# Whole token loads, a new order of the first key products, and w1's column means from rounded parts, in a one-core attention and mixer kernel

## The chip, the core and the metric

The kernel runs on one core of a Trainium2 chip. The metric is the device time of one execution in microseconds (us). The kernel before takes 523.48 us, the median of three runs (523.04 to 523.54).

The core has five engines that run their own instruction queues and meet at semaphores: TensorE (PE in the profile; PEld are its weight loads), VectorE (DVE), ScalarE (ACT), GpSimd (POOL) and SyncE (SP). SP and POOL also issue the DMA transfers between memory and the core's on-chip buffers; TensorE writes to accumulation banks (PSUM), which VectorE and ScalarE read.

## The reference

Two blocks read the same normalized tokens; one gates the other. There are S = 2048 tokens of D = 512 features, 32 heads of 16, and F = 1376 hidden features.

```python
xn = layernorm(x)
# A: linear attention
q, k, v = split(xn @ wqkv)
pq, pk = phi(q), phi(k)          # phi(t) = t + 1 if t > 0 else exp(t), plus 1e-6
kv  = einsum("bhsd,bhse->bhde", pk, v);  z = sum over s of pk
s   = (pq @ kv / (pq . z + 1e-6)) @ wo
# B: token mixing by shifts, then an MLP
h   = gelu(layernorm(xn) @ w1)   # its four column groups shifted by +1, -1, +2, -2 tokens
x1  = xn + shifted(h) @ w2
b   = x1 + gelu(layernorm(x1) @ w3) @ w4
out = x + s * silu(b)
```

## The kernel before

**Precision and tiling.** Tokens are cut into 16 tiles of 128, four tiles to a block of 512; the 512 features are cut into four chunks of 128. Nearly all products are made from rounded parts: a matrix a is split into hi (a rounded to the fp32r format, `rounded` at L478 or `Weights.split` at L552; usually ScalarE's copy) and lo (a - hi, VectorE's subtraction), and a product is the sum of hi*hi, hi*lo and lo*hi (`products`, L470): three TensorE instructions for each chunk. A product of unrounded values (`slow=True`) is one instruction that TensorE runs in two passes.

**A planner, not a scheduler of the chip, orders the work.** The code first records every operation with `Plan.add`. `Plan.emit` (L267) then lays them out in time by a table of assumed costs and emits them; the order of each engine's queue is what it decides. It works from due times (`deadlines`, L240, and `backward`, L261, which for a load takes an assumed latency off its user's due time; `PATIENCE` is the slack of operations that touch PSUM). The last lines of the kernel nudge single operations (the table `SOONER`, pairs of an operation's number and quarters of a microsecond) and set how early an operation may take a buffer (`lead`, `reserve`) and how far TensorE's order may depart from the order of recording (`window`, `ahead`).

**The start (L1176 to L1222).** TensorE runs WARM = 3 products of ones (`warm`), then one product of ones and zeros (`k<-zacc,ones`) that opens the bank of tile 0. The weights wk of the keys are loaded chunk by chunk (`wk_s`), chunk 0 in two halves of 256 columns. The tokens of block 0, transposed (`xt`), are loaded by `load_u(0, 2)` in two halves of 256 tokens: for every chunk first the half that holds tiles 0 and 1, later the half of tiles 2 and 3. Each half is rounded into u_0h to u_3h and u_0l to u_3l (the number is the chunk). The key products of tiles 0 and 1 begin with chunk 0 unrounded (`raw_k`, L670, tile 0 in two column halves), so that they need not wait for the rounding. Then come chunk 0 for tiles 2 and 3, chunks 1, 2, 3 for tiles 0 and 1, `ksum` (the column sums of wk, a product with ones of VectorE's three-step sum wkt), and chunks 1 to 3 for tiles 2 and 3.

`feature_k` (L738) makes phi(k): VectorE subtracts the mean's part (kt, with wneg, ScalarE's negative of ksum), ScalarE makes relu and exp (kr, kt), VectorE joins them (kr), ScalarE rounds (k0h for tile 0), VectorE takes the rest (k0l). `gram` (L774) then accumulates x^T phi(k) over all tiles in four banks g. The mean and variance of the first four tiles come from two ScalarE passes (sq) over the row-wise tokens x. `WQ.center` (L565) subtracts the column means from the query weights: VectorE sums the four chunks (wqt), one unrounded product with ones spreads the sum (wqm), and VectorE subtracts it from each chunk (wq_s), which is then rounded (wq_0h, wq_0l and so on) for `query`.

`W1.center(by_dma=True)` does the same for the mixer's w1, but the sum w1t is made by a load and three accumulating loads of the POOL queue; the product is w1m.

**The rest** (block by block the mixer, its second product, the MLP with seven products instead of eight per pair of halves, the attention's readout and the gate) is not touched by name, though the planner orders it anew.

**Queues.** SP issues all plain loads and stores in one queue. It uses eight semaphores in turn, so that its ninth transfer waits until the first has landed. POOL issues the accumulating transfers.

Of the kernel before, what the change touches and what calls it, by code (L numbers as in the profile page):

```python
# [14 lines left out]
P = 128  # L15
# [70 lines left out]
class Plan:  # L86
# [138 lines left out]


    GAP = .06
    PATIENCE = 2.5
    COLD, COLD_TILL = 1.84, 5.8
    SAFE = 2.0  # L230
    early = 0.0
# [8 lines left out]
    def deadlines(self, first):  # L240
# [8 lines left out]
        for op in self.ops:  # L249
# [3 lines left out]
            elif any(t.psum for t in op.tiles):  # L253
                op.due = min(op.due, op.at + self.PATIENCE)
            elif op.soon:
# [5 lines left out]
    def backward(self):  # L261
        for op in reversed(self.ops):
            if op.eng != "PE":
                for o in op.post:
                    op.due = min(op.due, o.due - self.GAP - (5.0 + op.mb * 4 if op.mb else op.lat))

    def emit(self, first, lead, reserve, window, ahead, table=()):  # L267
        self.deadlines(first)
# [125 lines left out]
def linear_attn_gated_by_mixer(  # L394
# [18 lines left out]
    NC = D // P  # L413
    NT = S // P
    QT = 4
    NQ = NT // QT
    BT = QT * P
# [1 line left out]
    W = 4  # L419
    SHIFT = (-1, 1, -2, 2)  # L420
    ORDER = (0, 2, 1, 3)
    WARM = 3
    PIECE = BT + W
    EARLY = (), ()
    AHEAD = 30.0, 20.0, 10.0, 0.0, 0.0
    TH = BT // 2
# [11 lines left out]
    pl = Plan(nc, pools, counts, ("acc", "mm"))  # L438

    def piece(name, dt=F32):  # L440
        return pl.new("p", name, dt, PIECE)[:, :512]

    def rounds(name):

        return piece(name + "h", F32R), piece(name + "l", F32R)
# [4 lines left out]
    def bank(name):  # L450
        return pl.new("mm", name, F32, 512)[:, :]

    def fixed(name, n, dt=F32):

        t = pl.new("const", name, dt, n)
        t.ap = const.tile([P, n], dt, name=name)
        return t
# [9 lines left out]
    def split(out, full, hi):  # L467
        pl.tt(out, full, hi.f32, ALU.subtract)

    def products(ps, terms, start=True, stop=True, more=False, behind=None):  # L470

        ms = []
        for sh, sl, mh, ml in terms:
            ms += [(sh, mh), (sh, ml), (sl, mh)]
        for n, (s, m) in enumerate(ms):
            pl.mm(ps, s, m, start and n == 0, stop and n == len(ms) - 1, more=more, behind=None if n else behind)

    def rounded(hi, lo, full, src=None):  # L478

        pl.act(hi, src or full, AF.Copy)  # L480
        split(lo, full, hi)
# [9 lines left out]
    ident, ones, nhalf, zacc = fixed("ident", P), fixed("ones", P), fixed("nhalf", QT), fixed("zacc", 512)  # L491
    identr = fixed("identr", P, F32R)
    onesr, bmask, tiny, zmore = fixed("onesr", P, F32R), fixed("bmask", P), fixed("tiny", 1), fixed("zmore", 1)
# [39 lines left out]
    X, XT = {}, {}  # L533
# [5 lines left out]
    class Weights:  # L539


        def __init__(self, name, src, parts=1):

            self.name, self.src = name, src
            self.raw = [piece(f"{name}_s{c}") for c in range(NC)]
            for c in range(NC):
                n = 1 if c else parts
                for k in range(n):
                    cs = k * 512 // n, (k + 1) * 512 // n
                    pl.load(self.raw[c].cols(*cs), src[:, c, cs[0]:cs[1]])  # L550

        def split(self, shared=0):  # L552
            self.hl = [rounds(f"{self.name}_{c}") for c in range(NC)]
# [11 lines left out]
        def center(self, by_dma=False):  # L565

            t, r = piece(self.name + "t"), self.raw
            if by_dma:
                pl.load(t, self.src[:, 0])
                for c in range(1, NC):  # L570
                    pl.gather(t, self.src[:, c])
            else:
                pl.tt(t, r[0], r[1], ALU.add)
                pl.tt(t, t, r[2], ALU.add)
                pl.tt(t, t, r[3], ALU.add)
            ps = bank(self.name + "m")
            pl.mm(ps, ones.all, t, True, True, slow=True)
            for c in range(NC):
                pl.stt(r[c], ps, -1.0 / D, r[c], ALU.mult, ALU.add)

# [15 lines left out]
    def scale_x(lo, n):  # L596

        r = rs1[:, lo:lo + n]
        w = small(f"w{lo}", n).all
        pl.ts(w, var(mv1, lo, lo + n), EPS, None, ALU.add, eng="POOL")  # L600
        power(r, w, n)
        pl.ts(ns1[:, lo:lo + n], r, -1.0, None, ALU.mult, eng="POOL")
        pl.tt(nm1[:, lo:lo + n], means(mv1, lo, lo + n), ns1[:, lo:lo + n], ALU.mult, eng="POOL")
        for i in range(lo, lo + n):
            halves_x(i)
# [25 lines left out]
    UT = {}  # L631

    def load_u(b, parts):

        n = BT // parts
        UT[b] = [[pl.new("p", f"u{b}_{c}{k}", F32R, PIECE) for k in "hl"] for c in range(NC)]
        for q in range(parts):
            o = q * n
            for c in range(NC):
                if q == 0:  # L640
                    XT[b, c] = piece(f"xt{b}_{c}")
                src = XT[b, c].cols(o, o + n)
                pl.load(src, xt[b, c][:, o:o + n])
                hi, lo = (t[:, 2 + o:2 + o + n] for t in UT[b][c])
                if b == c == q == 0:
                    pl.ts(hi, src, 1.0, None, ALU.mult)
                    split(lo, src, hi)
                else:
                    rounded(hi, lo, src)
# [12 lines left out]
    def ut(b, c, a, z):  # L662
        return tuple(t[:, a:z] for t in UT[b][c])

    def project(ps, i, ws, cs):
        b, j = divmod(i, QT)
        a = 2 + j * P
        products(ps, [ut(b, c, a, a + P) + ws.chunk(c) for c in cs], 0 in cs, NC - 1 in cs)

    def raw_k(ps, i):  # L670

        v = XT[0, 0].cols(i * P, (i + 1) * P)
        if i:
            pl.mm(ps, v, WK.raw[0], True, False, slow=True)
        else:
            for k in range(2):
                cs = k * TH, (k + 1) * TH
                pl.mm(ps.cols(*cs), v, WK.raw[0].cols(*cs), False, False, slow=True)

    def sum_k(ps):  # L680

        t, r = piece("wkt"), WK.raw
        pl.tt(t, r[0], r[1], ALU.add)
        pl.tt(t, t, r[2], ALU.add)
        pl.tt(t, t, r[3], ALU.add)
        pl.mm(ps, ones.all, t, True, True, slow=True)
# [51 lines left out]
    def feature_k(i, ps):  # L738

        t, r = piece(f"kt{i}"), piece(f"kr{i}")  # L740
        pl.stt(t, wneg.all, mean(mv1, i), ps, ALU.mult, ALU.add)
        pl.act(r, t, AF.Relu, scale=col(rs1, i))
        pl.act(t, t, AF.Exp, scale=col(rs1, i))
        hi, lo = rounds(f"k{i}")
        pl.stt(r, t, 1.0, r, ALU.min, ALU.add)
        pl.act(hi, r, AF.Identity, bias=tiny.all)
        pl.stt(lo, r, TINY, hi.f32, ALU.add, ALU.subtract)
        pl.gather(zacc.all, r)
        GK[i] += (hi, lo)

    def key(i):
        ps = bank(f"k{i}")
        project(ps, i, WK, range(NC))
        feature_k(i, ps)
# [421 lines left out]
    warm = bank("warm")  # L1176
    for n in range(WARM):
        pl.mm(warm.cols(n % NC * P, (n % NC + 1) * P), ones.all, ones.all, True, True, slow=True)
    ks = [bank("k0")]
    pl.mm(ks[0], ones.all, zacc.all, True, False, slow=True)  # L1180

    wneg = fixed("wneg", 512)
    G = [pl.new("acc", f"g{c}", F32, 512) for c in range(NC)]
# [12 lines left out]
        pl.act(t, X[i], AF.Square, bias=s.cols(1, 2), total=v)  # L1196
        pl.ts(v, v, 1.0 / D, None, ALU.mult)

    WK = Weights("wk", wqkv[1], 2)
    load_u(0, 2)  # L1200
    WK.split(1)
    for i in range(QT):
# [1 line left out]
    scale_x(0, 1)  # L1204
    scale_x(1, 1)
    scale_x(2, 2)
    ks[1:] = [bank(f"k{i}") for i in range(1, QT)]
    ksum = pl.new("acc", "ksum", F32, 512).all
    for i in range(2):
        raw_k(ks[i], i)  # L1210
    for i in range(2, QT):
        project(ks[i], i, WK, [0])
    for c in range(1, NC):
        for i in range(2):
            project(ks[i], i, WK, [c])
    sum_k(ksum)
    pl.act(wneg.all, ksum, AF.Copy, scale=-1.0)
    for i in range(2):
        feature_k(i, ks[i])
    for i in range(2, QT):  # L1220
        project(ks[i], i, WK, range(1, NC))
        feature_k(i, ks[i])  # L1222
    WQ = Weights("wq", wqkv[0])
    WQ.center()
# [73 lines left out]
    b = NQ - 1  # L1298
# [6 lines left out]
    for base, s in ((0, 1), (DH - 1, -1)):  # L1305
        v = bmask.all.via(lambda ap: ap.rearrange("p (h d) -> p h d", d=DH))
# [16 lines left out]
    for gg in range(NC):  # L1323
        cs = gg * P, (gg + 1) * P
        ps = bank(f"kv{gg}").cols(0, P)
# [4 lines left out]
    for gg in range(NC):  # L1330
        ps = bank(f"m{gg}")
# [10 lines left out]
    for b in range(NQ):  # L1342
# [50 lines left out]
        else:  # L1393
# [3 lines left out]
            t = piece(f"xi{i}", F32R)  # L1397
# [13 lines left out]
                gate(b * QT + QT - 1, a, o, D // 2, late=True, by_dma=False, whole=o > 0)  # L1411

    SOONER = (
# [7 lines left out]
    )  # L1421
    pl.emit(first=6.0, lead={"p": 12.0, "w": 10.0, "ab": 10.0}, reserve={"p": 8, "w": 1, "ab": 0}, window=7.0,
            ahead=3.0, table=SOONER)


# [35 lines left out]
```

## Time and profile before

| | |
|---|---|
| median of three runs | 523.48 us |
| the profiled execution: its own time | 523.29 us |
| its span, first to last instruction | 521.5 us |
| moved by DMA | 100.11 MB, mean 192 GB/s |
| TensorE instructions | 3011 |

One execution was profiled, and 1.8 us of its time lie around the span. In the lines shown below a group or instruction is named by source line, engine, operation and out<-in with buffer numbers left out; since every operation is recorded in a helper, the line is that of the helper, and the names tell what it is. Busy time of PE counts overlapping instructions once, and a matmul's recorded duration reaches past the start of the next, so what one costs is read from the starts. In a list by time, brackets hold the engine's idle time before the instruction and what ended it. SPq is the issue of a DMA from SP's queue.

### The profile page before, as it was taken

What the parts mean: (1) busy time and instruction counts of PE and PEld (TensorE: products, weight loads), DVE (VectorE), ACT (ScalarE), POOL (GpSimd) and SP (SyncE); (2) the same over time, 40 slices, a digit from 0 to 9 for tenths busy, and PEclk for the clock granted to TensorE, in tenths of its full rate; (3) what the DMA queues carried; (4) which work ended last, traced back from release to release, by engine and by line L of the source; (5) the groups of instructions that cost most, each with busy time, mean ns of one, the idle gap of its engine ahead of it and who ended that gap; (6) DMA issues with size and microseconds to landing.
All of it is one profiled execution on the core that took longest, in us unless ns stands there. A gap on an engine that the chain in (4) does not pass through costs nothing.

```text
span 521.5 us, 8876 instructions
## 1 busy us (share of the span) xinstructions
PE 514.3 (99%) x3011; PEld 445.8 (85%) x3011; DVE 375.0 (72%) x748; ACT 328.7 (63%) x669; POOL 112.2 (22%) x207
## 2 busy tenths in 40 slices
PE   8999999999999999999999999999999999999996
PEld 5777788988888888898999889899898898999985
DVE  4974697559475837899998458886567867496635
ACT  5899784769558837769865656466463456544621
POOL 1777253140272022211100022000040000310000
PEclk9999999999999999999999999999999999999999
DMA  7959993375887189999685969848489466898704
GB/s 239 291 126 200 225 234 81 79 165 186 184 197 168 34 192 240 268 242 264 232 265 183 264 161 202 266 134 203 119 172 313 147 182 129 200 288 251 230 1 121
DMA packets 73856, 100.11 MB, mean 192 GB/s; under 512 B 7908, under 2 KB 31988, under 8 KB 73812
## 3 DMA queue, kind: packets, MB, share of 16 engines
q1 hardware_dynamic: 62724, 79.37, 49.5%
q0 software_dynamic: 11088, 20.19, 23.4%
q8 instruction: 23, 0.38, 0.3%
q14 instruction: 21, 0.17, 0.1%
HBM read 60.33 MB, written 30.81 MB: 175 GB/s over the span
## 4 chain that ended last, share of the span: by engine, by line
PE 93%; ACT 3%; DMA 2%; SPq 1%; DVE 1%; issue 1%; DVEq 0%; ACTq 0%
PE acc L146 23%; PE pb L146 11%; PE h L146 9%; PE g L146 8%; PE q L146 8%; PE pe L146 6%; PE k L146 5%; PE pbm L146 4%; PE pbs L146 3%; PE pa L146 3%; PE pem L146 2%; PE s L146 2%; PE a L146 2%; PE pes L146 2%; DMA wk_s<-in_wqkv 1%; PE pam L146 1%
## 5 line engine op out<-in xcount | busy, mean ns | idle before, releaser
L223 POOL DMA_DIRECT2D xo<-x1d x12 | 10.7, 1179 | 166.6 <-ACT xo L167 166.6
L223 POOL DMA_DIRECT2D th<-in_x x14 | 12.1, 868 | 72.2 <-DVE th L199 51.4
L167 ACT ACTIVATE p<-pb 128x256 f32<-128x256 f32 x20 | 7.7, 383 | 31.5 <-PE pb L146 31.4
L223 POOL DMA_DIRECT2D zacc<-kr x16 | 15.4, 963 | 52.4 <-DVE kr L199 43.5
L223 POOL DMA_DIRECT2D o<-x x16 | 14.6, 930 | 41.8 <-ACT o L167 19.9
L167 ACT ACTIVATE gf<-gf 128x256 f32<-128x256 f32 (+1 forms) x40 | 20.9, 523 | 0.9
L199 DVE SCALAR_TENSOR_TENSOR kt<-wneg,mv,k 128x512 f32<-128x512 f32 x16 | 11.8, 745 | 11.2 <-PE k L146 11.1
L167 ACT ACTIVATE ht<-ht 128x512 f32<-128x512 f32 x16 | 10.0, 630 | 15.5 <-DVE ht L189 15.5
L223 POOL DMA_DIRECT2D pqd<-qe x16 | 15.0, 938 | 19.6 <-DMA pqd<-qr 5.2
L199 DVE SCALAR_TENSOR_TENSOR kr<-kt,kr 128x512 f32<-128x512 f32 x16 | 11.1, 691 | 10.7 <-ACT kt L167 10.6
L167 ACT ACTIVATE th<-xo 128x512 f32<-128x512 f32 (+1 forms) x16 | 9.8, 616 | 13.4 <-DVE xo L189 11.7
L167 ACT ACTIVATE p<-pe 128x256 f32<-128x256 f32 x20 | 7.7, 384 | 12.3 <-PE pe L146 12.3
L189 DVE TENSOR_TENSOR gf<-pa,p 128x256 f32<-128x256 f32 x20 | 8.4, 422 | 9.3 <-ACT p L167 4.8
L189 DVE TENSOR_TENSOR ht<-h,abc 128x512 f32<-128x512 f32 x16 | 10.7, 687 | 5.8 <-PE h L146 5.3
L167 ACT ACTIVATE qe<-q,ns 128x512 f32<-128x512 f32 x16 | 10.9, 681 | 5.5 <-PE q L146 5.5
L167 ACT ACTIVATE x<-x,nm,rs 128x512 f32<-128x512 f32 x16 | 12.3, 807 | 3.2 <-POOL nm L189 3.2
L167 ACT ACTIVATE kr<-kt,rs 128x512 f32<-128x512 f32 x16 | 11.5, 717 | 3.6 <-DVE kt L199 3.5
L588 DVE BATCH_NORM_STATS2 st<-o 128x6 f32<-128x512 f32 x16 | 10.8, 686 | 3.2 <-DMA o<-x 3.2
L189 DVE TENSOR_TENSOR gf<-u,pe 128x256 f32<-128x256 f32 x20 | 8.3, 416 | 6.3 <-PE pe L146 6.3
L199 DVE SCALAR_TENSOR_TENSOR th<-th,so 128x512 f32<-128x512 f32 (+1 forms) x17 | 11.1, 658 | 2.3 <-ACT th L167 1.4
L167 ACT ACTIVATE y<-o,nm,rs 128x512 f32<-128x512 f32 x16 | 12.2, 802 | 0.0
L167 ACT ACTIVATE kt<-kt,rs 128x512 f32<-128x512 f32 x16 | 11.6, 724 | 0.4
(1567 smaller groups left out, 2195.0 us busy)
## 6 DMA issues: line engine op xcount, KB each, us to landing
w_s<-in_w SPq DMA_DIRECT2D x28, 256.0 KB, 4.4
x<-in_x SPq DMA_DIRECT2D x16, 256.0 KB, 5.1
zacc<-kr POOLq DMA_DIRECT2D x16, 256.0 KB, 5.3
pqd<-qr SPq DMA_DIRECT2D x16, 256.0 KB, 3.2
pqd<-qe POOLq DMA_DIRECT2D x16, 256.0 KB, 5.4
o<-x POOLq DMA_DIRECT2D x16, 256.0 KB, 4.8
x1d<-o SPq DMA_DIRECT2D x16, 256.0 KB, 4.0
pq<-pqd SPq DMA_DIRECT2D x16, 256.0 KB, 4.4
```

The costliest lines, as they stand in the source:

```text
L146: lambda: nc.tensor.matmul(out.get(), lhs.get(), rhs.get(), start=start, stop=stop, skip_group_check=more))
L167: nc.scalar.activation(out.get(), src.get(), func, scale=get(scale), **kw)
L189: self.vec(eng, out, [a, b], lambda: self.e(eng).tensor_tensor(out.get(), a.get(), b.get(), op=op), True)
L199: lambda: self.nc.vector.scalar_tensor_tensor(out.get(), a.get(), get(s), b.get(), op0=op0, op1=op1),
L223: lambda: self.nc.gpsimd.dma_start(out.get(), get(src), accum_op=ALU.add), mb=mb)
L588: pl.add("DVE", .62, .69, [xv], [st], lambda: nc.vector.bn_stats(st.get(), xv.get()))
```

## The change

Three edits in the program and new constants for the planner.

1. **Loads.** wk's chunk 0 is loaded in one piece. Of block 0's tokens only chunk 0 is still loaded and rounded in two halves; chunks 1, 2 and 3 are loaded whole (512 tokens) and rounded whole.
2. **Order of the first key products.** The product of ones and zeros is gone, tile 0's raw product is one instruction, and WARM is 8. Chunk 1 is multiplied for all four tiles in turn, ahead of chunks 2 and 3 for tiles 0 and 1; tiles 2 and 3 take chunks 2 and 3 at the end.
3. **w1's means.** The sum w1t is rounded into hi and lo, and two rounded products take the place of the unrounded one.
4. **Planner.** PATIENCE 5.0 for 2.5, an assumed load latency of 6.0 for 5.0, other `reserve`, `window` and `ahead`, and another table.

```diff
-    PATIENCE = 2.5
+    PATIENCE = 5.0
...
-                    op.due = min(op.due, o.due - self.GAP - (5.0 + op.mb * 4 if op.mb else op.lat))
+                    op.due = min(op.due, o.due - self.GAP - (6.0 + op.mb * 4 if op.mb else op.lat))
...
-    WARM = 3
+    WARM = 8
...
-                n = 1 if c else parts
-                for k in range(n):
-                    cs = k * 512 // n, (k + 1) * 512 // n
-                    pl.load(self.raw[c].cols(*cs), src[:, c, cs[0]:cs[1]])
+                pl.load(self.raw[c], src[:, c])
...
-            pl.mm(ps, ones.all, t, True, True, slow=True)
+            if by_dma:
+                ts = rounds(self.name + "m")
+                rounded(*ts, t)
+                for n, v in enumerate(ts):
+                    pl.mm(ps, onesr.all, v, n == 0, n == 1)
+            else:
+                pl.mm(ps, ones.all, t, True, True, slow=True)
...
+                if c and parts > 1:
+                    if q == 0:
+                        pl.load(XT[b, c], xt[b, c])
+                        rounded(*(t[:, 2:2 + BT] for t in UT[b][c]), XT[b, c])
+                    continue
...
-                if b == c == q == 0:
+                if b == q == 0 and parts > 1:
...
-        v = XT[0, 0].cols(i * P, (i + 1) * P)
-        if i:
-            pl.mm(ps, v, WK.raw[0], True, False, slow=True)
-        else:
-            for k in range(2):
-                cs = k * TH, (k + 1) * TH
-                pl.mm(ps.cols(*cs), v, WK.raw[0].cols(*cs), False, False, slow=True)
+        pl.mm(ps, XT[0, 0].cols(i * P, (i + 1) * P), WK.raw[0], True, False, slow=True)
...
-    ks = [bank("k0")]
-    pl.mm(ks[0], ones.all, zacc.all, True, False, slow=True)
...
-    WK = Weights("wk", wqkv[1], 2)
+    WK = Weights("wk", wqkv[1])
...
-    for c in range(1, NC):
-        for i in range(2):
-            project(ks[i], i, WK, [c])
+    for i in range(QT):
+        project(ks[i], i, WK, [1])
+    for i in range(2):
+        project(ks[i], i, WK, [2])
+    for i in range(2):
+        project(ks[i], i, WK, [3])
...
-        project(ks[i], i, WK, range(1, NC))
+        project(ks[i], i, WK, [2, 3])
...
-    pl.emit(first=6.0, lead={"p": 12.0, "w": 10.0, "ab": 10.0}, reserve={"p": 8, "w": 1, "ab": 0}, window=7.0,
-            ahead=3.0, table=SOONER)
+    pl.emit(first=6.0, lead={"p": 12.0, "w": 10.0, "ab": 10.0}, reserve={"p": 20, "w": 1, "ab": 0}, window=6.0,
+            ahead=6.0, table=SOONER)
```

In the program that is built, the SP queue begins with wk_s (chunk 0), xt_0 in two halves, xt_2, wk_s (chunk 1), xt_1, x0, wk_s (chunk 2), xt_3, wk_s (chunk 3), and then the four chunks of wq_s with x1 ahead of the last. Before, it begins with xt_0's first half, wk_s (chunk 0) in two halves, xt_0's second half, xt_1's first half, wk_s (chunk 1), xt_2's first half, wk_s (chunk 2), x0, wk_s (chunk 3), xt_3's first half, x1, and xt_1's second half.

TensorE's queue begins with eight warm products, the raw products of tiles 0 and 1, chunk 0 of tiles 2 and 3, chunk 1 of all tiles, chunk 2 of tiles 0 and 1, the first product of chunk 3 for tiles 0 and 1, ksum, the rest of chunk 3 for tiles 0 and 1, twelve products of chunks 2 and 3 for tiles 2 and 3, wqm and the gram of tile 0.

More of the change, by code (lines that the diff above doesn't have):

```diff
@@ L539, in linear_attn_gated_by_mixer, with __init__ @@
     class Weights:
-        def __init__(self, name, src, parts=1):
+        def __init__(self, name, src):
             self.name, self.src = name, src
@@ L1206, in linear_attn_gated_by_mixer @@
     scale_x(2, 2)
-    ks[1:] = [bank(f"k{i}") for i in range(1, QT)]
+    ks = [bank(f"k{i}") for i in range(QT)]
     ksum = pl.new("acc", "ksum", F32, 512).all
```

12 rows, old and new, of the table SOONER are left out of this document.

## The prediction

> **What bounds the kernel now.** I read the page first, then the busy time by stretch, then the first 25 us instruction by instruction, TensorE's order first and then the work it waits for.
>
> ```profile
> span 521.5 us, 8876 instructions
> PE 514.3 (99%) x3011; PEld 445.8 (85%) x3011; DVE 375.0 (72%) x748; ACT 328.7 (63%) x669; POOL 112.2 (22%) x207
> PE 93%; ACT 3%; DMA 2%; SPq 1%; DVE 1%; issue 1%; DVEq 0%; ACTq 0%
> ```
>
> TensorE is busy 99% of the span and is 93% of the chain that ended last. By stretch (length; busy us and instructions of PE, PEld, DVE, ACT, POOL; granted clock; DMA share; GB/s):
>
> ```profile
> 0.00:10.00 10.00, 8.65 (x26) 5.64 (x26) 3.47 (x8) 4.19 (x9) 2.26 (x14) 1.00 0.70 197
> 10.00:20.00 10.00, 8.94 (x34) 5.67 (x32) 8.95 (x22) 9.19 (x22) 4.94 (x11) 1.00 0.94 313
> 30.00:40.00 10.00, 10.00 (x45) 8.11 (x44) 7.37 (x17) 9.76 (x17) 8.90 (x16) 1.00 0.70 146
> 40.00:60.00 20.00, 20.00 (x89) 16.02 (x88) 9.24 (x15) 18.14 (x33) 9.51 (x26) 1.00 1.06 242
> 200.00:250.00 50.00, 50.00 (x318) 44.01 (x317) 45.94 (x98) 39.58 (x86) 11.75 (x16) 1.00 0.95 258
> ```
>
> After 20 us TensorE has no idle worth naming. Time is to be had only in the first 20 us, or by taking work off TensorE. Its order there (start, duration; in brackets its idle and who ended it):
>
> ```profile
> 1.12 1.65 PE L146 MATMUL warm<-ones 128*128 128x128 f32 x6 [1.12 <-POOL ones L503]
> 2.56 1.91 PE L146 MATMUL k<-zacc,ones 128*128 128x512 f32 x2
> 4.27 2.52 PE L146 MATMUL k<-wk_s,xt 128*128 128x256 f32 x6
> 6.85 0.40 PE L146 MATMUL k<-wk_0l,u_0h 128*128 128x512 f32 x1
> 8.86 0.50 PE L146 MATMUL k<-wk_1l,u_1h 128*128 128x512 f32 x1 [0.23 <-DVE wk_1l L189]
> 10.52 0.50 PE L146 MATMUL k<-wk_2h,u_2h 128*128 128x512 f32 x1 [0.22 <-ACT wk_2h L167]
> 13.07 0.50 PE L146 MATMUL k<-wk_3h,u_3h 128*128 128x512 f32 x1 [0.41 <-ACT u_3h L167]
> 14.61 1.02 PE L146 MATMUL ksum<-wkt,ones 128*128 128x512 f32 x2
> 15.69 0.39 PE L146 MATMUL k<-wk_1l,u_1h 128*128 128x512 f32 x1
> 19.39 0.40 PE L146 MATMUL k<-wk_3h,u_3l 128*128 128x512 f32 x1
> 20.11 1.10 PE L146 MATMUL wqm<-wqt,ones 128*128 128x512 f32 x2 [0.32 <-DVE wqt L189]
> 43.59 0.40 PE L146 MATMUL k<-wk_0h,u_0h 128*128 128x512 f32 x1
> 60.53 1.02 PE L146 MATMUL w1m<-w1t,ones 128*128 128x512 f32 x2
> ```
>
> A rounded 512-wide product costs (19.39-15.69)/16 = 0.231 us from start to start. An unrounded one is two passes: ksum starts at 14.61, the second product behind it at 15.69, so it costs 1.08-0.231 = 0.85. From 6.85-0.23 = 6.62 to wqm at 20.11 lie 13.49 us; the 42 rounded products and ksum need 10.56. So 2.9 us are lost, waiting for chunks 1, 2 and 3 and for wqt. That is the most the new order can win.
>
> **TensorE's start.** The change drops the zero-filling product and adds five 128-wide ones. Half a zero-filling product is a pass of (4.27-2.56)/2 = 0.855; a 128-wide pass is a quarter, 0.214. Ten passes more than the first six: 2.56+2.14 = 4.70. wk's first block (now one load of 256 KB) and the first tokens are 384 KB; so many had landed before at
>
> ```profile
> 4.50 0.29 DVE L194 TENSOR_SCALAR wk_0h<-wk_s 128x256 fp32r<-128x256 f32 x1 [4.50 <-DMA wk_s<-in_wqkv]
> ```
>
> which is in time. The raw products, 1.71 us at full rate, took 4.27 to 6.62 = 2.35: 0.64 were lost to half rate, so full rate came 1.28 us after 4.27, at 5.55. From 4.70, 0.85 us at half rate do 0.425; the remaining 1.285 end at 6.83, then six products of chunk 0 end at 8.22. Before: 6.62 and 8.01. So 0.2 later.
>
> The clock row grants full clock throughout the first stretch, while the rows show half rate until 5.55. The Trainium skill (TensorE: Matmul & The Clock Gate, Part 1: The HAM clock gate) says that the clock opens after about 3.4 us of activity, counted in time and not in products, in a window that runs free of the kernel's start. By that rule five more warming products buy nothing and the switch could come elsewhere; the time from 1.12 to 5.55 agrees as far as one run can, and with the switch at 5.55 in both kernels the sum stays as it is. The rival on the clock is this rule's.
>
> **The loads of chunk 1.** Chunk 1's products for tiles 0 to 3 need u_1h, now rounded from xt_1 whole. The landings of before are read off ScalarE, whose roundings wait for them:
>
> ```profile
> 5.46 0.42 ACT L167 ACTIVATE u_1h<-xt 128x256 fp32r<-128x256 f32 x1
> 7.44 0.63 ACT L167 ACTIVATE wk_1h<-wk_s 128x512 fp32r<-128x512 f32 x1 [1.56 <-DMA wk_s<-in_wqkv]
> 8.32 0.42 ACT L167 ACTIVATE u_2h<-xt 128x256 fp32r<-128x256 f32 x1 [0.25 <-DMA xt<-in_xt]
> 9.84 0.63 ACT L167 ACTIVATE wk_2h<-wk_s 128x512 fp32r<-128x512 f32 x1 [1.09 <-DMA wk_s<-in_wqkv]
> 10.54 0.63 ACT L167 ACTIVATE sq<-x 128x512 f32<-128x512 f32 x1
> ```
>
> These are the 5th to 9th loads of SP's queue: xt_1's half, wk_1, xt_2's half, wk_2, x0. Bytes up to each: 640, 896, 1,024, 1,280 and 1,536 KB. In the changed queue wk_1 is the 5th and xt_1 the 6th, with 1,280 KB up to it. If the count sets the pace, xt_1 lands at 7.44; if the bytes do, at 9.84. Neither law fits alone: the 256 KB of wk_1, wk_2 and x0 took 1.98, 1.52 and 0.70, so the early slowness passed with time. I take the middle, 8.64, and likewise 9.43 for x0 (7th) and 10.5 for wk_2 (8th). All other first loads land before TensorE asks.
>
> **Sum to wqm.** u_1h is ready at 8.64+0.63 = 9.27: TensorE waits 1.05. Twelve products of chunk 1 end at 12.05. ScalarE does the two passes over x0 (9.43 to about 11.1), then wk_2h by 11.7; VectorE subtracts to wk_2l by 12.57 (0.69 after the wkt sum ahead of it). The second product of chunk 2 waits 0.3, to 12.6. Seven more to ksum at 14.2; ksum 0.85 and 16 products: wqm at 18.8, against 20.11: **-1.3**. Covers: wqt is VectorE's third sum, behind kt of tiles 0 and 1, which wait for wneg (ScalarE, 0.6 after ksum); it is done near 18.2, 0.6 ahead.
>
> **From wqm to tile 4's keys.** The same 97 products lie there, 0.85+96x0.231 = 23.06; before took 43.59-20.11 = 23.48, 0.42 lost. What feeds the gram products now (rows of before):
>
> ```profile
> 17.17 0.71 ACT L167 ACTIVATE kr<-kt,rs 128x512 f32<-128x512 f32 x1
> 17.91 0.72 ACT L167 ACTIVATE kt<-kt,rs 128x512 f32<-128x512 f32 x1
> 18.67 0.69 DVE L199 SCALAR_TENSOR_TENSOR kr<-kt,kr 128x512 f32<-128x512 f32 x1
> 19.68 0.70 ACT L167 ACTIVATE k0h<-kr,tiny 128x512 fp32r<-128x512 f32 x1
> 31.67 0.71 ACT L167 ACTIVATE k2h<-kr,tiny 128x512 fp32r<-128x512 f32 x1
> ```
>
> Tile 0: kt from 16.0 to 16.7, ScalarE's two functions to 18.4, kr to 19.1, k0h from 19.2 to 19.9: 0.25 after wqm's end at 19.65. The first wq_0l costs another 0.16, being the same chain behind wqm. Tile 2: before, ScalarE goes from k0h to k2h in 12.0 us. In the changed queue five more operations stand between the two (x1's second pass, x2's first, one qr, one qe, x2h: 0.72+0.62+0.57+0.57+0.52 = 3.0), and wq_3h stands directly behind wq_2h though VectorE centres its source only after three subtractions: ScalarE is held 1.6 there (23.3 to 24.9), against 0.6 in the old queue. So k2h starts at 19.2+12.0+3.0+1.0 = 35.2 and ends at 35.9; TensorE arrives after 65 products at 19.9+0.16+15.0 = 35.1. Cost 0.7; bounds 0 (the hold falls into waits) and 1.2 (ScalarE starts no earlier than before's 19.68). Loss 0.25+0.16+0.7 = 1.1 against 0.42: **+0.7**.
>
> **w1's means.** One unrounded product (0.85) becomes two rounded ones (0.46): **-0.4**, in a stretch where TensorE never idles. Price: one rounding of 0.63 on ScalarE, which has 1.86 us idle in 40 to 60, and 0.69 on VectorE, which has over 10. The rounding waits for the third accumulating load of w1, and x4h's successors queue behind it; before, that load was issued at
>
> ```profile
> 39.29 0.91 POOL L223 DMA_DIRECT2D w1t<-in_w  x1
> w1t<-in_w POOLq DMA_DIRECT2D x1, 256.0 KB, 5.8
> ```
>
> and would land at 45.1, while ScalarE reaches the rounding near 44. In the new POOL queue these loads stand ahead of more work, so I take nothing; the bound is 1.1.
>
> **The rest.** New planner constants reorder all queues, but at every hundredth TensorE instruction the two programs have issued ScalarE and VectorE within 8 instructions of each other, and 2,888 of 2,983 TensorE instructions keep their relative order. I take 0, bounds -0.4 and +0.6 (the largest loss seen after 20 us, at wqm, is half that).
>
> **Sum**: -1.3+0.7-0.4 = -1.0 on the profiled execution's 523.29, which is 0.19 under the median 523.48 and inside 523.04 to 523.54. Forecast 522.3.
>
> **Rivals.**
> 1. The count sets the loads' pace: xt_1 at 7.44, no wait for chunk 1: 1.05 less, 521.2. For it: 1 KB-wide halves moved only 128 KB per issue. Against: wk_1, the first load of 256 KB, took longer than any half.
> 2. The bytes do: xt_1 at 9.84, 1.2 later: 523.5, no change. For it: DMA busy 0.70 to 0.94 in these stretches. Against: the queue starts with wider rows.
> 3. Slower: one of the 16 lanes stalls under xt_1 as it did under wk_1 (1.5 late against the load before), on top of the bytes' pace: 11.3 instead of 8.64, each us of it one us of TensorE, 525.0. It decides from a landing at 10.7 on (0.2% slower); from 9.6 the gain is gone.
> 4. w1's rounding holds ScalarE 1.1, and k4h behind it reaches the gram late: 523.4.
> 5. Full rate comes only with chunk 1. Raw products 4.70+3.42 = 8.12, chunk 0 at 0.46 each to 10.9, 1.6 after u_1h: 523.9. The rule quoted above would allow it; the three runs lie within 0.5, which speaks against it.
> 6. Slower later: VectorE becomes the bound in 200 to 250. It has 4.06 us to spare; seven roundings of 0.6 pulled into it use that up, and five more make TensorE wait 3.0: 525.3. The counts above speak against it.
>
> **Chances.** 0.2% is 1.05 us, about what a measurement here can tell from no change: faster under 522.43, slower over 524.53. Forecast 0.42 (own range 521.6 to 523.0, from xt_1 between 7.9 and 9.3; somewhat over half lies under 522.43), rival 1 0.18, 2 0.17, 3 0.08, 4 0.05, 5 0.03, 6 0.07. Faster 0.24+0.18+0.01 = 0.43, slower 0.08+0.07 = 0.15, same the rest. The range 520.9 to 524.2 takes in rivals 1, 2, 4 and 5 with the rest's bounds and leaves out 3 and 6.
>
> **What would show it.** Chunk 0's last product near 8.0, a wait for u_1h of about 1 us, wqm near 18.8, ScalarE held before wq_3h, a wait of up to 0.9 before k2h, tile 4's first key product near 42.9, w1m as two rows 0.23 apart. Wrong would be: wk's whole first block later than 4.7, xt_1 outside 7.4 to 9.9, or an idle of over 0.5 after 60 us.

## The result, and the profile after

The changed kernel takes 522.21 us, the median of 10 runs (521.97 to 522.82); before took 523.58 beside it (10 runs, 522.88 to 524.24). The ratio is 0.9974, 95% interval 0.9965 to 0.9982: 1.37 us less, 0.26%. The profiled execution took 522.82 and is the slowest of the ten; against the profiled one of before (523.29) it is 0.47 less, so its rows understate the gain. The kernel was therefore profiled a second time (first experiment).

The page of the changed kernel: its span, and the shares of the chain that ended last, of which TensorE (PE) still holds 90%:

```profile
span 520.8 us, 8908 instructions
...
PE 90%; ACT 3%; DMA 3%; DVE 2%; issue 0%; SPq 0%; POOL 0%; POOLq 0%; DVEq 0%
```

Busy time by stretch (columns as before: length, PE, PEld, DVE, ACT, POOL, granted clock, DMA share, GB/s):

```profile
0.00:10.00 10.00, 7.96 (x29) 6.00 (x30) 3.42 (x7) 5.16 (x10) 2.24 (x14) 1.00 0.68 228
10.00:20.00 10.00, 9.91 (x40) 6.88 (x38) 9.25 (x21) 7.12 (x15) 5.01 (x10) 1.00 0.95 337
...
30.00:40.00 10.00, 9.57 (x42) 7.48 (x41) 6.58 (x17) 9.87 (x19) 7.82 (x15) 1.00 0.43 102
```

TensorE was idle in 10 to 20 before (8.94 busy of 10); now it is busy there (9.91), and 0.43 of idle has appeared in 30 to 40, where there was none. In 0 to 10 it is busy for 0.69 less (7.96 against 8.65). TensorE's order (start, duration; in brackets its idle and who ended it):

```profile
1.11 3.78 PE L146 MATMUL warm<-ones 128*128 128x128 f32 x16 [1.11 <-POOL ones L503]
5.08 2.21 PE L146 MATMUL k<-wk_s,xt 128*128 128x512 f32 x4 [0.19 <-DMA xt<-in_xt]
...
8.28 0.40 PE L146 MATMUL k<-wk_0h,u_0l 128*128 128x512 f32 x1
...
9.42 0.50 PE L146 MATMUL k<-wk_1h,u_1h 128*128 128x512 f32 x1 [0.74 <-ACT u_1h L167]
...
12.58 0.50 PE L146 MATMUL k<-wk_2l,u_2h 128*128 128x512 f32 x1
...
18.89 1.02 PE L146 MATMUL wqm<-wqt,ones 128*128 128x512 f32 x2
...
20.00 0.96 PE L146 MATMUL g<-k0h,x0h 128*128 128x512 f32 x3
...
36.02 1.20 PE L146 MATMUL g<-k2h,x2h 128*128 128x512 f32 x4 [0.43 <-ACT k2h L167]
...
43.34 0.40 PE L146 MATMUL k<-wk_0h,u_0h 128*128 128x512 f32 x1
...
60.25 0.39 PE L146 MATMUL w1m<-w1mh,onesr 128*128 128x512 f32 x1
...
60.95 0.40 PE L146 MATMUL q<-wq_0l,u_0h 128*128 128x512 f32 x1
...
515.72 0.28 PE L146 MATMUL accx<-w_9h,f_9l 128*128 128x256 f32 x1
```

The waits for chunks 2 and 3 and for wqt are gone. What is left at the start, behind the first tokens, is one wait for u_1h. A new wait stands before tile 2's gram products, for k2h. ScalarE's and VectorE's side of the two:

```profile
8.73 0.63 ACT L167 ACTIVATE u_1h<-xt 128x512 fp32r<-128x512 f32 x1 [0.72 <-DMA xt<-in_xt]
9.36 0.64 ACT L167 ACTIVATE sq<-x 128x512 f32<-128x512 f32 x1
...
24.96 0.63 ACT L167 ACTIVATE wq_3h<-wq_s 128x512 fp32r<-128x512 f32 x1 [1.52 <-DVE wq_s L199]
...
35.26 0.71 ACT L167 ACTIVATE k2h<-kr,tiny 128x512 fp32r<-128x512 f32 x1
```

```profile
17.58 0.69 DVE L189 TENSOR_TENSOR wqt<-wqt,wq_s 128x512 f32<-128x512 f32 x1
...
24.25 0.68 DVE L199 SCALAR_TENSOR_TENSOR wq_s<-wqm,wq_s 128x512 f32<-128x512 f32 x1
```

ScalarE stands at wq_3h for 1.52 us until VectorE has centred wq_s at 24.25, and k2h then starts at 35.26.

Where the time went, by the start of four TensorE products. Two rows of before that the prediction did not need:

```profile
61.62 0.40 PE L146 MATMUL q<-wq_0l,u_0h 128*128 128x512 f32 x1
...
516.68 0.27 PE L146 MATMUL accx<-w_9h,f_9l 128*128 128x256 f32 x1
```

| | before | after | difference | after, second profile | difference |
|---|---|---|---|---|---|
| wqm | 20.11 | 18.89 | -1.22 | 18.57 | -1.54 |
| tile 4's first key product | 43.59 | 43.34 | -0.25 | 43.00 | -0.59 |
| wq_0l behind w1m | 61.62 | 60.95 | -0.67 | 60.61 | -1.01 |
| last product | 516.68 | 515.72 | -0.96 | 515.03 | -1.65 |
| end of the span | 521.5 | 520.8 | -0.7 | 520.1 | -1.4 |

Won up to wqm: 1.2 to 1.5. Given back up to tile 4: 0.97 and 0.95. Won at w1m: 0.42 twice. Won later: 0.29 and 0.64. Lost behind the last product: 0.27 twice (5.06 us from its start to the end of the span, 4.79 before). A further 0.16 lies outside the span: a run's time less its span is 1.97 in the median of the changed kernel's 21 runs, 1.81 in before's.

### The profile page after: what moved, and what is told of

Read it like the earlier page. It is cut to its first block, busy times and chain, and to the rows that moved or that the text cites. A ratio compares the mean times of both kernels' runs of the same rounds, so it can differ in the third digit from the quotient of the medians.

```text
span 520.8 us, 8908 instructions
## 1 busy us (share of the span) xinstructions
PE 513.3 (99%) x3017; PEld 446.4 (86%) x3017; DVE 375.4 (72%) x746; ACT 330.7 (63%) x667; POOL 110.5 (21%) x207
## 4 chain that ended last, share of the span: by engine, by line
PE 90%; ACT 3%; DMA 3%; DVE 2%; issue 0%; SPq 0%; POOL 0%; POOLq 0%; DVEq 0%
PE acc L146 22%; PE pb L146 10%; PE h L146 9%; PE g L146 8%; PE k L146 7%; PE q L146 7%; PE pe L146 5%; PE pbm L146 4%; PE pbs L146 3%; PE pa L146 2%; PE pem L146 2%; PE s L146 2%; PE pes L146 2%; PE a L146 2%; DMA xo<-x1d 2%; PE pam L146 1%
## 5 line engine op out<-in xcount | busy, mean ns | idle before, releaser
L199 DVE SCALAR_TENSOR_TENSOR qz<-pq,zb 128x512 f32<-128x512 f32 x16 | 10.8, 681 | 2.6 <-PE acc L146 2.6
```

The lines of the kernel that those rows point to most:

```text
L199: lambda: self.nc.vector.scalar_tensor_tensor(out.get(), a.get(), get(s), b.get(), op0=op0, op1=op1),
```

## The experiments

Theory: the start gains what the new order and the landings of xt_1 and wk_2 allow; ScalarE, held at wq_3h, gives part of it back at k2h; w1m gives 0.4; the rest is nearly neutral. Rivals: the planner's new order of the later stages makes the time, not the named edits; full rate of TensorE depends on the warming products; each microsecond of xt_1's landing is one of TensorE's.

**The changed kernel again** (no edit).

> The changed kernel as it is, a second time, to learn how well its rows repeat. If the landings are set by the queue and not by chance, xt_1's rounding starts within 0.2 us of 8.73, wqm within 0.2 of 18.89, tile 4's first key product within 0.2 of 43.34, and the last TensorE product starts near 515.7. If one lane's chance stall made the 8.73, xt_1 moves by over 0.5 and wqm with it. Time against before: 1.2 to 1.4 us less.

522.29 us (11 runs), ratio 0.9979, 0.9971 to 0.9988: 1.0 us under the 523.28 of before beside it, not the 1.2 to 1.4 expected.

```profile
7.93 0.63 ACT L167 ACTIVATE u_1h<-xt 128x512 fp32r<-128x512 f32 x1
...
8.62 0.50 PE L146 MATMUL k<-wk_1h,u_1h 128*128 128x512 f32 x1 [0.16 <-ACT u_1h L167]
...
18.57 1.02 PE L146 MATMUL wqm<-wqt,ones 128*128 128x512 f32 x2
...
43.00 0.40 PE L146 MATMUL k<-wk_0h,u_0h 128*128 128x512 f32 x1
...
515.03 0.28 PE L146 MATMUL accx<-w_9h,f_9l 128*128 128x256 f32 x1
```

The same program rounds xt_1 0.80 earlier. Six later kernels with the same loads up to there (experiments 4 to 8 and 11) round it at 7.86, 7.97, 7.88, 7.84, 8.14 and 8.48. So a landing is good to within 0.9 us, not to 0.2 as expected, and 8.73 is the latest of eight. wqm follows by only 0.32, since other operands are late next: TensorE loses about 0.4 around its first products with u_1l and 0.1 before wk_2l. Differences of 0.3 in a start's row between two profiles mean nothing; times do, where their intervals allow.

**xt_1 loaded ahead of xt_2.** The table's due times of the two are exchanged, and two VectorE operations held in order:

```diff
-    ..., 27, 842, 30, 870, ...
+    ..., 27, 858, 30, 842, 31, 8, ...
+    after=((46, 176),)
```

> Of the changed kernel only the order of two loads is turned round: xt_1 goes 4th and xt_2 6th (one pair of operations on VectorE is held in its old order). Theory (a wait that is removed hands over to the next late operand): u_1h is ready before wk_1h, and wk_1h, near 8.0, before chunk 0 ends at 8.5, so the wait of 0.7 for u_1h is gone; but wk_2, still the 8th load, is split on ScalarE and VectorE only by 12.5, so TensorE waits 0.6 to 0.9 in chunk 2 instead, wqm stays within 0.2 of 18.89 and the time within 0.3 us of the changed kernel's. Rival (each microsecond of xt_1's landing is one of TensorE's, as the prediction's third rival had it): wqm near 18.2 and 0.5 to 0.7 us less time.

522.17 us (12 runs, 521.81 to 523.87), ratio 0.998: 0.12 under the repeated kernel, so the theory's "within 0.3" held and the rival's 0.5 to 0.7 did not come. The plan did not keep to the two loads, though: TensorE's order differs from the changed kernel's at 15 places, 11 of them after 60 us, so the 0.12 is not the price of the loads alone. The profiled execution happened to be the one of 523.87, and shows something else:

```profile
5.45 3.75 PE L146 MATMUL k<-wk_s,xt 128*128 128x512 f32 x4 [0.55 <-DMA xt<-in_xt]
...
20.06 1.02 PE L146 MATMUL wqm<-wqt,ones 128*128 128x512 f32 x2
...
516.80 0.28 PE L146 MATMUL accx<-w_9h,f_9l 128*128 128x256 f32 x1
```

Here the tokens were 0.37 later (5.45 against 5.08), TensorE paused for 0.55 behind the warming products, and the raw products ran at half rate to their end (3.75 for the group instead of 2.21). wqm and the end are 1.5 to 1.8 later than in the second profile: 523.87 against 522.05 for that execution. Because of it the wait in chunk 2 could not be read from these rows; the ninth experiment tests it again.

**Chunks 1 to 3 in halves again** (with the table moved on by the nine added operations).

```diff
-                if c and parts > 1:
-                    if q == 0:
-                        pl.load(XT[b, c], xt[b, c])
-                        rounded(*(t[:, 2:2 + BT] for t in UT[b][c]), XT[b, c])
-                    continue
```

> Of the changed kernel only the loads of chunks 1 to 3 are halved again, as before (xt_1's two halves go 6th and 7th, wk_2 9th; two pairs of operations are held in their old order). If whole loads are what made the start faster, u_1h is ready later than 9.4, or the second halves hold tiles 2 and 3, and wqm comes after 19.5. If the loads' bytes set the pace, xt_1's first half (1,024 KB up to it instead of 1,280) is there near 8.0, TensorE waits less than 0.3 for chunk 1, and what it wins is lost again at wk_2: wqm between 18.6 and 19.3 and the time within 0.4 us of the changed kernel's.

526.04 us (6 runs, 524.77 to 527.8), ratio 1.005: 3.8 more than the changed kernel. wqm came after 19.5, as the first expectation had it; neither had the time.

```profile
1.12 3.39 PE L146 MATMUL warm<-ones 128*128 128x128 f32 x16 [1.12 <-POOL ones L506]
...
8.45 0.71 ACT L167 ACTIVATE u_1h<-xt 128x256 fp32r<-128x256 f32 x2
...
8.90 0.50 PE L146 MATMUL k<-wk_1h,u_1h 128*128 128x512 f32 x1 [0.72 <-ACT u_1h L167]
...
20.07 1.12 PE L146 MATMUL wqm<-wqt,ones 128*128 128x512 f32 x2 [0.52 <-DVE wqt L189]
...
45.00 0.40 PE L146 MATMUL k<-wk_0h,u_0h 128*128 128x512 f32 x1
...
521.17 0.28 PE L146 MATMUL accx<-w_9h,f_9l 128*128 128x256 f32 x1
```

xt_1's half, 128 KB, was rounded at 8.45, later than the whole 256 KB in six of the eight executions named above (7.84 to 8.73 in all). So half the bytes won nothing here; with landings that vary by 0.9, one execution does not show that bytes never count. Tile 4 is 1.7 to 2.0 late. But from tile 4 to the last product another 3.8 to 4.1 are lost (476.17 against 472.38 and 472.03), in stages that the edit does not name. The profiled execution, 527.80, is the slowest of the six and 1.8 over their median, so these rows overstate the loss.

**The key products written down as before.**

```diff
-    for i in range(QT):
-        project(ks[i], i, WK, [1])
-    for i in range(2):
-        project(ks[i], i, WK, [2])
-    for i in range(2):
-        project(ks[i], i, WK, [3])
+    for c in range(1, NC):
+        for i in range(2):
+            project(ks[i], i, WK, [c])
...
-        project(ks[i], i, WK, [2, 3])
+        project(ks[i], i, WK, range(1, NC))
```

> Of the changed kernel only the order in which the key products are written down is as before (chunks 1 to 3 for tiles 0 and 1, then for 2 and 3). If that order carries the gain of the start, as the prediction's sum has it, six products less stand ahead of chunk 2, TensorE waits about 1.4 for wk_2h and wqm starts near 20.3. Rival: the planner, whose window is 6 us, pulls products of tiles 2 and 3 forward by itself (three of tile 2's and one of tile 3's chunk 1 stand ahead of wk_2l in the built order), TensorE waits under 0.3 in chunk 2, and what delays wqm is wqt, whose third sum now stands behind tile 0's kr on VectorE: wqm near 19.85. Either way the wait before k2h gives most of it back: tile 4's first key product between 43.3 and 43.9, time 0 to 0.5 us more than the changed kernel's.

525.59 us (5 runs), ratio 1.004: 3.3 more, against 0 to 0.5 expected. The waits of TensorE in this kernel:

```profile
PE pe L146 <- ACT p L167: 0.9, 2, 0.7
PE wqm L146 <- DVE wqt L189: 0.6, 1, 0.6
...
PE pb L146 <- DVE gf L189: 0.4, 1, 0.4
```

At the start it went the rival's way: no wait in chunk 2, 0.6 for wqt, wqm at 19.25 (the rival had 19.85), tile 4 at 43.86. From there to the last product 2.6 to 2.9 are lost. The pe and pb rows are part of it, behind 200 us: the MLP's products wait for ScalarE and VectorE, and TensorE idles 1.65 us between 200 and 500, where the changed kernel has 0.12 to 0.19. The edit names operations of the first 20 us only, but the planner ordered the later queues anew, with a table of due times tuned for another order: TensorE's order differs from the changed kernel's at 60 places, 48 of them after 60 us (61 and 48 in the third experiment). So a time of this experiment or the third is not the price of its edit. From here on the planner's final list was taken as it stands and single operations moved in it, with every other queue as in the changed kernel:

```diff
-            op.emit()
+            line.append(op)
...
+        for op in edited(line):
+            op.emit()
```

**The order of the key products alone**, by such an edit: in TensorE's places for products 103 to 164, those of tiles 0 and 1 first, then ksum, then tiles 2 and 3.

> The changed kernel with every engine's instructions in its own order, but for TensorE's key products of chunks 1 to 3: first those of tiles 0 and 1, then ksum, then those of tiles 2 and 3, as the list before had them. No other order moves, so later stages can differ only by what this hands on. Theory (this order carries the gain of the start): six products less stand ahead of chunk 2, TensorE waits about 1.3 us for wk_2h and 0.5 for wk_2l, ksum starts near 14.8 instead of 13.99, wqm near 20.3 instead of 18.57 to 18.89; part is covered by the wait before k2h, and the time is 0.9 to 1.4 us more than the changed kernel's 522.2. Rival (the order hardly counts, the loads and the plan of the later stages do): wqm within 0.5 of 18.9 and the time within 0.3.

523.92 us (11 runs), ratio 1.0008, 0.9999 to 1.0016: 1.6 to 1.7 more than the changed kernel, over the 0.9 to 1.4 expected; of the changed kernel's gain nothing is left that the interval shows.

```profile
9.88 0.50 PE L190 MATMUL k<-wk_1h,u_1l 128*128 128x512 f32 x1 [0.49 <-DVE sx L238]
...
11.31 0.50 PE L190 MATMUL k<-wk_2h,u_2h 128*128 128x512 f32 x1 [0.24 <-ACT wk_2h L211]
...
12.20 0.51 PE L190 MATMUL k<-wk_2l,u_2h 128*128 128x512 f32 x1 [0.39 <-DVE wk_2l L233]
...
20.30 1.02 PE L190 MATMUL wqm<-wqt,ones 128*128 128x512 f32 x2
...
44.30 0.40 PE L190 MATMUL k<-wk_0h,u_0h 128*128 128x512 f32 x1
...
516.75 0.28 PE L190 MATMUL accx<-w_9h,f_9l 128*128 128x256 f32 x1
```

Chunk 1 waits 0.49 for u_1l, which VectorE has ready at 9.82 (the row names sx, VectorE's next), and chunk 2 for wk_2h and wk_2l. With the changed order, products of other tiles stand in these places. wqm is at 20.30 as expected, and tile 4 1.0 to 1.3 late. From tile 4 to the end it takes 472.45, as in the changed kernel. TensorE's order differs from the changed kernel's at five places here, none after 60 us. So the order is what carries the start.

**w1's means from one unrounded product.** The rounding of the sum and its difference are left out.

> The changed kernel, all orders kept, with w1's column means from one unrounded product again; the rounding of the sum and its difference are left out. Theory: TensorE never idles there, so the time is 0.4 us more than the changed kernel's (0.85 against 0.46), and the product after w1m starts 0.4 later. Rival (the rounding that is gone holds ScalarE, or a later wait takes the time up): no difference, within 0.2.

```profile
59.85 1.02 PE L596 MATMUL w1m<-w1t,ones 128*128 128x512 f32 x2
...
60.93 0.39 PE L153 MATMUL q<-wq_0l,u_0h 128*128 128x512 f32 x1
```

From w1m to wq_0l it takes 1.08 instead of 0.70: 0.38, as forecast. The time is 522.38 (10 runs), ratio 0.9978, 0.9969 to 0.9987: 0.1 to 0.2 more than the changed kernel. The median lies where the rival had it, and the interval holds both 0.4 and nothing; the row decides for the place, the time decides nothing. From wq_0l to the last product this execution takes 454.52, as the changed kernel does (454.77 and 454.42), so nothing there takes the 0.38 up again.

**Three warming products.**

```diff
-    WARM = 8
+    WARM = 3
```

> The changed kernel, all orders kept, with 3 warming products instead of 8, so that TensorE idles from about 2.8 us to the first raw product near 5.1. Theory of the prediction (five more warming products buy nothing; full rate comes near 5.6 anyhow): the raw products end near 6.8, wqm and the time as in the changed kernel, within 0.3. Rival (full rate comes only after a stretch of work without such a pause, as the one profiled execution of the second experiment shows, where a pause of 0.55 put it off to about 9.8): raw products at half rate up to 8.5, chunk 0 in part too, wqm near 20.1 and the time 1.4 to 1.8 us more.

523.49 us (11 runs, 522.28 to 524.06), ratio 0.9995, 0.9986 to 1.0004: 1.2 to 1.3 more. The rival held in kind, a little under its 1.4 to 1.8, with wqm at 19.70 for its 20.1.

```profile
5.14 3.75 PE L150 MATMUL k<-wk_s,xt 128*128 128x512 f32 x4 [2.38 <-DMA xt<-in_xt]
...
19.70 1.02 PE L150 MATMUL wqm<-wqt,ones 128*128 128x512 f32 x2
```

The raw products run at half rate throughout, as in the one execution of the second experiment.

**ScalarE's hold filled.** Pairs are an operation and the one it goes behind; 63 and 69 are the second passes over x2 and x3, 188 is wq_2h.

```diff
+MOVES = ((63, 188), (69, 63), (62, 187), (68, 62), (64, 58), (70, 64))
```

> The changed kernel with six operations moved and every other order kept: x2's and x3's second passes on ScalarE go ahead of wq_3h, into the 1.5 us in which ScalarE is held there, and the four small VectorE operations that feed and follow them move up with them. Theory (ScalarE's hold before wq_3h is what k2h is late by): k2h starts 1.0 to 1.3 us earlier, near 34.1, TensorE's wait of 0.6 before tile 2's gram products is gone, 0.1 to 0.2 is lost to the moved VectorE operations, tile 4's first key product comes 0.4 to 0.6 earlier and the time is 0.3 to 0.6 us less than the changed kernel's 522.2. Rival (k2h waits for something else, such as tile 2's scale from GpSimd, or the time is lost again later): k2h not before 34.9 and the time within 0.2.

521.74 us (5 runs), ratio 0.9961, 0.9947 to 0.9974: 0.5 under the changed kernel.

```profile
25.18 0.62 ACT L206 ACTIVATE wq_3h<-wq_s 128x512 fp32r<-128x512 f32 x1
...
34.06 0.71 ACT L206 ACTIVATE k2h<-kr,tiny 128x512 fp32r<-128x512 f32 x1
```

k2h starts 1.20 earlier than in the first profile of the changed kernel and 0.90 earlier than in the second, and its row is gone from TensorE's waits. Tile 4 is at 42.89: from wqm it takes 24.13, and 24.11 in the repeat below, against 24.45 and 24.43. So the hold is the cause of the wait before k2h, and filling it is worth 0.3 in the rows; the medians gained 0.5, and what the other 0.2 is, the rows do not show.

**The start fed.** wk_2's rounding goes ahead of x0's second pass as well, so that the next late operand of the second experiment comes sooner.

```diff
+MOVES = ((26, 35), (27, 36), (30, 41), (29, 20), (28, 37), (43, 48), (44, 127), (52, 44), (128, 52),
+         (54, 45), (75, 131), (76, 134), (25, 132))
```

> The changed kernel with thirteen operations moved in the first 18 us and every other order kept: xt_1 is loaded 4th and xt_2 after wk_1, their roundings and differences follow that order, wk_2's rounding goes ahead of x0's second pass on ScalarE, wk_2l ahead of the second sum of wk, wneg ahead of x0's scaling, x0h behind tile 0's two functions. Theory (the second experiment won nothing because wk_2, behind x0's two passes, was the next late operand): with both moved, TensorE waits under 0.3 in chunks 1 and 2, ksum starts near 13.4 to 13.6 (13.9 to 14.3 in the changed kernel), wqm near 18.0 and the first gram product 0.3 to 0.5 earlier; ScalarE still reaches k2h late, so the wait there stays 0.4 to 0.7 and the time is 0.2 to 0.5 us less than the changed kernel's 522.2. Rival (k2h is bound by ScalarE's total work and not by what comes before it): the gain is lost at k2h, and the time is within 0.15.

521.92 us (5 runs), ratio 0.9966, 0.9952 to 0.998: 0.3 less, within the theory's 0.2 to 0.5. But the interval takes in nearly all of the changed kernel's (0.9965 to 0.9982), so the gain is not shown. The profiled execution was the slowest of the five (522.41), with a late full rate:

```profile
4.99 3.04 PE L185 MATMUL k<-wk_s,xt 128*128 128x512 f32 x4
...
13.91 1.02 PE L185 MATMUL ksum<-wkt,ones 128*128 128x512 f32 x2
...
35.65 1.20 PE L185 MATMUL g<-k2h,x2h 128*128 128x512 f32 x4 [0.41 <-ACT k2h L206]
```

No wait stands in chunks 1 and 2, but ksum is 0.3 to 0.5 later than expected because chunk 0 itself was slow (raw products in 3.04 instead of 2.21); the wait for k2h is still there.

**Both, and the filled hold again.** The nineteen moves together; and the eighth kernel a second time.

> The thirteen moves of the ninth experiment and the six of the eighth together. Theory: the two gains are of different places and add up: no wait of over 0.3 before 60 us but for the first load, tile 4's first key product near 42.3, the time 0.7 to 1.0 us less than the changed kernel's 522.2, so 521.2 to 521.5. Rival (the later stages wait for VectorE or the loads and give it back): no faster than the eighth experiment's 521.7.

> The kernel of the eighth experiment once more, beside the tenth on one chip. Theory: 521.6 to 521.9, 0.3 to 0.6 under the changed kernel's 522.2 as before. If the first 5 runs were a lucky draw, 522.0 to 522.3.

521.59 us for both (5 runs, 521.05 to 521.85), ratio 0.9963, 0.995 to 0.9975; 521.74 for the filled hold (ratio 0.9966). In the rows of the first:

```profile
4.92 1.95 PE L185 MATMUL k<-wk_s,xt 128*128 128x512 f32 x4 [0.20 <-DMA xt<-in_xt]
...
42.25 0.39 PE L185 MATMUL k<-wk_0h,u_0h 128*128 128x512 f32 x1
...
514.38 0.28 PE L185 MATMUL accx<-w_9h,f_9l 128*128 128x256 f32 x1
```

Full rate came early in this execution (the raw products took 1.95), which helped. Tile 4 is at 42.25 as expected and the last product 0.65 to 1.3 before the changed kernel's. In time it is 0.6 to 0.7 less, short of the 0.7 to 1.0 expected, and the 0.15 between these two kernels is less than their intervals, so the rival (no faster than the filled hold) stands. Both are faster than before, by 1.6 to 1.8 us. Against the changed kernel the medians are lower each time, by 0.5 to 0.7; the runs were not taken beside it, and the ratios' intervals overlap.

## Why the prediction was right, point by point

**TensorE's start.** Forecast: raw products from 4.70, chunk 0's last near 8.0. Measured: 5.08 and 8.28. The step that failed is "which is in time": the 384 KB that TensorE needs first were there by 4.50 before, but the tokens came behind wk's whole first block and TensorE waited for them. It cost nothing in the sum, since u_1h came later still. That the switch to full rate would be at 5.55 in both kernels was luck: it was at 5.54 and 5.60 in the two profiled executions, but between 3.96 and 7.19 in ten executions with the same eight warming products (see the last section). The step "five more warming products buy nothing" is wrong: with three, the time is 1.2 to 1.3 us more. What it overlooked is the zero-filling product, which kept TensorE at work up to the raw ones in the kernel before; it is gone, and the eight products take its place.

**The loads of chunk 1.** xt_1 and x0 were forecast at 8.64 and 9.43; their users started at 8.73 and 9.36. But 8.73 is the latest of eight executions with these loads, the others being at 7.84 to 8.48, five of them below 8.0: the middle of the two laws was met by luck, and most landings lie between it and the first rival's 7.44. None came near the second rival's 9.84. Counted from the starts, as the forecast's 1.05 was, TensorE waited 0.91 and, in the second profile, 0.32. Up to wqm the sum held all the same, because an earlier xt_1 moved wqm less than the forecast's range had it.

**wqm** at 18.8 forecast, 18.89 and 18.57 measured. The new order carries it (fifth experiment): this is the step that holds the gain, and it was forecast by its mechanism. The wqt cover held: VectorE's third sum ended at 18.27, against 18.2 forecast.

**From wqm to tile 4** the sum had +0.7, the rows show +0.97 and +0.95. Every named term stands: k0h 0.26 (from 19.74 to 20.00), ScalarE's hold 1.52 against 1.6, k2h at 35.26 against 35.2, the wait before it 0.59 against 0.7 (36.02 less 35.43, where TensorE arrived). Mis-sized is what is not named: of 24.45 us, 23.06 are products and about 1.0 are the named waits; the remaining 0.4 are spread over 97 products, and no row puts them to a wait. So the first product of tile 4 came at 43.34, not 42.9.

**w1's means** gave 0.42 in both profiles against 0.4, and the sixth experiment 0.38 the other way. The third accumulating load kept nobody waiting: TensorE is busy for 20.00 of the 20 us from 40 to 60, and the fourth rival falls.

**The rest** was put at 0 with bounds -0.4 and +0.6; it gave -0.29 and -0.64 up to the last product. Behind it 0.27 was lost in the span and 0.16 outside, which the prediction did not look at. Together that is between +0.1 and -0.2, within the bounds, but as effects that offset each other. Which of the planner's new orders won it was not tried. That they are worth microseconds the third and fourth experiments show: the same table behind another start loses 2.6 to 4.1 us from tile 4 on. The prediction's count of kept orders (2,888 of 2,983) said that little moved; it could not say whether the little mattered, and 0 was luck as much as reading.

**The sum**, -1.0, stands against -0.5 between the two profiled executions, -1.24 for the second profile's (522.05) and -1.0 to -1.4 in the medians. The start and w1m carry it as forecast. Three sizes that were off offset one another: the loss before tile 4 was 0.3 larger, the end of the kernel 0.4 longer, the later stages 0.3 to 0.6 shorter. **Rival 5** (late full rate, 523.9) is a real mechanism: the one execution of 523.87 in the second experiment is that case. Among 21 runs of the changed kernel none was above 522.87, so its small chance was fair. **Rival 3**, each microsecond of xt_1 one of TensorE's, does not hold for earlier landings: 0.80 of landing moved wqm by 0.32; a landing later than 8.73 was not seen. The reading behind it was off too: it was not one of the 16 lanes that stalled under wk_1 before, since of that load's sixteen landings eight came from 5.96 to 6.20 and eight from 7.04 to 7.42. **Rival 6** did not come: VectorE is busy 45.8 of 50 us in 200 to 250, as before (45.9).

## What to carry to other kernels

When a wait is removed at the start, name the next late operand before counting the gain: here moving xt_1 ahead won nothing that can be told from noise, and filling the hold that made k2h late won 0.3 in the rows. Where a planner orders the queues from a tuned table, undo an edit in its finished list, not in its input, or the experiment prices the table. Products that only keep TensorE at work belong to the start as much as loads do, and one that looks useless may keep TensorE busy until full rate comes. One profile's row is one draw: what agrees with a forecast in one execution can lie at the edge of what the same program does.

## What the runs showed of the hardware

**One and the same start reaches full rate at moments 3.2 us apart.** Each trace holds a record of the granted clock, and in all thirteen it begins where the distance between TensorE's starts falls to half, so it gives the moment. With eight warming products from 1.11 or 1.12 us on and pauses of at most 0.39 behind them, it was at 3.96, 4.26, 4.40, 5.02, 5.14, 5.34, 5.60, 6.36, 6.95 and 7.19. The rows show it too. In the first three of these the warming products themselves end early (the group lasts 3.39, 3.54 and 3.60 instead of 3.78). The raw products' group lasts 1.95 to 1.98 where they run at full rate throughout or but for the start of the first, and 2.12, 2.21, 2.58, 2.94 and 3.04 where full rate comes during them. In the two executions with a pause of 0.55 and 2.38 it lasts 3.75, half rate throughout, and full rate came at 10.00 and 9.51, which is 4.55 and 4.37 after TensorE resumed. The column of the granted clock reads 1.00 in the stretch from 0 to 20 in all of them that were read, since the record begins only with the full rate; so the column does not show the slow start.

The Trainium skill (TensorE: Matmul & The Clock Gate, Part 1: The HAM clock gate) says that the clock opens after a busy window of about 3.4 us which runs free of the kernel's start. These runs agree with it as far as they go: the ten moments spread over nearly one such window, and the pauses put full rate off beyond all ten. They differ in one point: 3.96 is only 2.84 after the first product, so a window that opened the clock there was not busy from end to end. One execution stands for the pause of 0.55, so how short a pause may be stays open.

**The first loads' landings wander.** Eight executions with the same loads rounded xt_1 at 7.84 to 8.73, and in the one with half its bytes at that place it was no sooner (8.45). Early in the kernel neither bytes nor count gave a landing to better than about 0.9 us.
